# An attention-and-experts kernel: the first list's indices right behind their table's product, the next expert's gathers ahead of the puts

## The chip, the core and the metric

The kernel runs on one core of a Trainium2 chip, as one launch. The metric is the device time of that launch in microseconds (us). All tensors are drawn from a normal distribution, so which tokens go to which expert is known only while the kernel runs.

## The reference, cut to what matters

```python
# retention attention, batch 4, 8 heads, 768 steps, width 64
state = gamma * state + outer(k[t], v[t]);  y[t] = q[t] @ state / sqrt(64)
x = y as [3072, 512]
# mixture of experts, 8 experts, hidden width 1024
noisy = x @ w_gate + log1p(exp(x @ w_noise)) * noise
top2 = the two largest of noisy per token;  g = softmax over the two
for e in range(8):
    out[rows of e] += g * (relu(x[rows of e] @ w1[e]) @ w2[e])
```

What has to be computed is thus a causal recurrence over 768 steps for 32 head-batches, then a gate that sends each of the 3072 rows of x to two of eight experts, and for each expert two matrix products over its own rows.

## The kernel before, in words

**Stage one: attention.** Time is cut into chunks of 128 steps, 6 per batch, 24 in all. The loop over j at L677 handles one chunk per turn and is written so that several chunks are in flight. In turn j, TensorE gets the score products of the next chunk (`qk(j+1)`, L305), then what is listed for the turn in `between`, then the output products of this chunk (`y_mm(j)`, L320) and the gate logits of chunk j-3 (L360). VectorE scales the finished chunk j-1 in two halves (`x_hi` L345, `x_lo` L350) and multiplies the next chunk's scores by the causal mask (`masked`, L315). GpSimd scales v (`v_scale`, L282) and q (`q_scale`, L288). SyncE issues the loads, and for a finished chunk a transposing DMA and a store of its rows into `xbuf` (`x_out`, L354).

**Routing, hidden in the loop.** After each batch of 6 chunks its routing runs in steps (`route_a` to `route_g`), put into the turns by the lists `between` (before `y_mm`) and `todo` (behind it), filled at L634 to L670. `route_h` (L447) splits the gate values in two bf16 parts, `route_d` (L454) makes each token's slot, `route_e` one-hot matrices. `table(b)` (L507) multiplies them on TensorE, which gives each slot's token and gate in the PSUM region `LST`. `route_f` (L514) adds `LST` to `acc`, `slots` (L522) turns columns of `acc` into the row indices `idx`. `route_g` (L565) keeps copies of gates and places for a loop that serves overflowing lists at the end. `LST`, the places `POS` and the small sums `SUM` are regions of one PSUM tile, `pR` (L144 to L149). A Tile framework writes all semaphore waits; each engine's own order is the order of the calls.

**Weights of the first expert.** `w_load` to `w_lo` (L168 to L203) load one expert's weights, sum their squares on ScalarE, derive a scale (`w_scale`, a TensorE product into `SUM`, L184, and a VectorE reduction), and split them into two fp16 halves: ScalarE the upper (`w_hi`), VectorE the lower (`w_lo`), or ScalarE and GpSimd (`w_lo_pool`, L205). For expert 0 these steps are in the lists too.

**Stage two: experts.** `gather(e, t)` (L617) has GpSimd fetch 128 rows of `xbuf` by the indices, into one of four `xg` buffers; `x_t(e, t)` (L629) has SyncE issue the transposing DMA into `xe`, which waits for the gather. `mm1` (L716) is a first-product unit of 12 matmuls, with a relu on ScalarE and a remainder on VectorE; `mm2` (L748) a second-product unit of 24 matmuls; `put` (L742) has GpSimd add the scaled result `ot` to `out` by an indirect DMA. Puts go one behind the other: each waits for the landing of the one before. `ot` has four buffers.

**Expert 0 goes in pieces.** Its first list of 384 rows can only hold tokens of the first two batches, so its three gathers are possible once `route_f(1)` is done; they are in turns 21 and 22. When the loop is over, TensorE runs first-list units between the last routing steps (`early`, L787): eight `mm1` on 384 columns, three `mm2`, then eight `mm1` on columns 384 to 576, and one more `mm2`. At L840 four puts are issued; then SyncE reads the order of the other experts (L843) and issues 4 MB of loads for the next one (L844 to L846). The loop over experts starts at L849. For e = 0 it runs eight `mm1` on columns 576 to 832; `ahead` (L855) holds the seven gathers with transposes of the next expert, popped one per unit from the fifth unit on (L875) and then ahead of each `mm2` (L884).

Of the kernel before, what the change touches and what calls it, by code (L numbers as in the profile page):

```python
# [19 lines left out]
B, H, S, D = 4, 8, 768, 64  # L20
C = 128
NC = S // C
NCH = B * NC
# [11 lines left out]
B0 = B // 2  # L35
# [59 lines left out]
def moe_kernel(ctx, tc, qT, kT, kt, vt, noise, wgn, w1, w2, ctab, qtab, xbuf, out):  # L95
# [511 lines left out]
    def at(j, f, *a):  # L607
        todo.setdefault(j, []).append((f, a))
# [25 lines left out]
    between = {}  # L634
    for b in range(B - 1):
        n = (b + 1) * NC
        steps = [(2, route_a, b), (3, route_b, b), (4, route_b2, b), (4, route_c, b), (5, route_h, b), (5, route_d, b),
                 (6, route_e, b, 0), (7, route_e2, b, 0), (7, route_e, b, 1), (8, route_e2, b, 1), (9, route_f, b),
                 (8 if b == 0 else NCH - 1 - n, route_g, b)]
        if b == B - 2:  # L640
            steps = [(2, route_a, b), (3, route_b, b), (3, route_b2, b), (4, route_c, b), (4, route_h, b), (5, route_d, b)]
        else:
            between.setdefault(n + 9, []).append((table, b))
        between.setdefault(n + 5, []).append((places, b))
        for s in steps:
            at(n + s[0], *s[1:])
    at(0, gate_sum)
    at(1, gate_weights)
    for i in range(4):
        at((4, 7, 10, 12)[i], w_load, 0, "1", i)  # L650
        at((6, 9, 12, 14)[i], w_sum, 0, "1", i)
        at((15, 16, 17, 18)[i], w_hi, 0, "1", i)
        at((18, 19, 20, 20)[i], w_lo, 0, "1", i)
        at((14, 16, 17, 18)[i], w_load, 0, "2", i)
        at((16, 18, 19, 20)[i], w_sum, 0, "2", i)
        at(21 + i // 2, w_hi, 0, "2", i)
# [3 lines left out]
    between.setdefault(21, []).append((w_scale, 0, "2"))  # L660
    at(22, w_lo_pool, 0, "2", 0)
    between[NCH - 1].append((w_lo_pool, 0, "2", 1))
    at(NC * (B0 + 1) + 3, slots, 0, 3)
    for t in range(3):
        at(NC * (B0 + 1) + 3 + t // 2, gather, 0, t, 0, 128, B0 * S)
        if t < 2:
            at(NC * (B0 + 1) + 4, x_t, 0, t)
    between[NCH - 1].append((x_t, 0, 2))
    mid = SECOND // 128
    at(1, nc.sync.dma_start, xbuf[:128, :], zero.bitcast(F16))  # L670
# [32 lines left out]
    x_hi(NCH - 1)  # L703
    x_lo(NCH - 1)
    x_out(NCH - 1)
    for i in range(7):
        zero_out(i)
    lctx.close()
# [128 lines left out]
        early(2)  # L837
    early(len(units))
    out_scale(0, mid, NBLK)
    for t in range(mid):  # L840
        put(0, t, first[t])
    for r in range(E - 1):
        order.append(nc.sync.value_load(eid[0:1, r:r + 1], min_val=1, max_val=E - 1))  # L843
    for w in "12":  # L844
# [4 lines left out]
    for e in range(E):  # L849
        half = (CAPS[e] + 31) // 32 * 16  # L850
        cols = [(SECOND, CAPS[0])] if e == 0 else [(0, half), (half, CAPS[e])]
        n, more = 0, e + 1 < E

        if more:
            ahead = [lambda t=t: (gather(e + 1, t), x_t(e + 1, t)) for t in blocks(e + 1)]  # L855
        for n0, n1 in cols:
            for f in range(FT):
                mm1(e, n0, n1, f)
                if tail is not None and n == 0:
                    put(*tail[:2], tail_out(*tail))  # L860
                    tail = None
                if e:
                    if n == 2:
                        w_scale(e, "2")
                        out_scale(e, 0, NBLK)
                    if 3 <= n < 7:
                        w_hi(e, "2", n - 3)
                    if 4 <= n < 8:
                        w_lo(e, "2", n - 4)
                    if more and n == 2:  # L870
                        w_load(e + 1, "1", 0, 2)
                        w_load(e + 1, "1", 2, 2)
                if more and len(cols) * FT - 5 <= n < len(cols) * FT - 1:
                    w_sum(e + 1, "1", n - (len(cols) * FT - 5))
                if e == 0 and n >= 4:  # L875
                    ahead.pop(0)()
                n += 1
        if more and e:
            w_load(e + 1, "2", 0, 2)
            w_load(e + 1, "2", 2, 2)  # L880
            w_scale(e + 1, "1")
        todo = list(range(mid, NBLK)) if e == 0 else list(blocks(e))
        for n, t in enumerate(todo):
            if more and ahead:  # L884
                ahead.pop(0)()
            if block(e, t)[1] < 128:
                tail = mm2_tail(e, t)
            else:
                put(e, t, mm2(e, t))
                if tail is not None:  # L890
                    put(*tail[:2], tail_out(*tail))
                    tail = None
            if e == 0 and n == 0:
                w_scale(1, "1")
            if more:
                for i in ((2 * n, 2 * n + 1) if e == 0 else (n,)):
                    if i < 4:
                        w_hi(e + 1, "1", i)
                    if 1 <= i < 5:
                        w_lo(e + 1, "1", i - 1)  # L900
                if e and 2 <= n < 6:
                    w_sum(e + 1, "2", n - 2)
            if e == 1 and n == 2:
                route_g(b - 1)
                route_g(b)
                loop_table()
        if e == 0:
            for i in range(4):
                w_sum(1, "2", i)
# [102 lines left out]
```

## Time and profile before

| | |
|---|---|
| median of 3 runs | 712.27 us (711.22 to 712.94) |
| the profiled execution, its own time | 716.62 us |
| its span, first to last instruction | 714.2 us |
| TensorE matmul busy | 672.1 us, 94% |
| VectorE, ScalarE, GpSimd busy | 296.2, 298.2, 216.2 us |
| mean granted TensorE clock | 0.964 of full speed |

The page of the profile gives the busy time of each engine, the span in 40 slices with the granted TensorE clock, and the chain of work that ended last. The trace behind it gives single instructions in order of time (the timeline), the idle time in front of groups of instructions and who ended it (the waits), and busy time and clock in chosen stretches (the windows). Times in these views count from the start of the span. Stage one lasts until about 142 us, the first-list units start at about 151 us, and the next expert's units at about 231 us.

### The profile page before, as it was taken

Reading aid. Unit: us, or ns where it says so; the run is one execution under the profiler, and the core shown is the slowest. Engines: PE = TensorE matmul, PEld = TensorE weight load, DVE = VectorE, ACT = ScalarE, POOL = GpSimd, SP = SyncE. Lnnn points to the kernel's source line nnn. Section 1 sums busy time; section 2 is a strip of 40 time slices with the busy share of each in tenths; the row PEclk is TensorE's granted clock in tenths of the full one; section 3 lists DMA queues with packets and bytes.
Section 4 is the critical chain, followed back from the end, with each engine's and each line's share of the span. In section 5 each row is a group of like instructions: output and inputs, shape, how many; then the busy total and the mean of one; then the engine's idle time right before and its main releaser. Section 6 shows DMA issues by size and latency. Waiting matters only on the chain.

```text
span 714.2 us, 11981 instructions
## 1 busy us (share of the span) xinstructions
PE 672.1 (94%) x4789; PEld 420.2 (59%) x4789; DVE 296.2 (41%) x731; ACT 298.2 (42%) x540; POOL 216.2 (30%) x170
## 2 busy tenths in 40 slices
PE   8999999859897999999999999999999999999991
PEld 6999898735674554555455545554554465456540
DVE  4457879867733343453216220622152144215100
ACT  4543454721146453444344442444353454344110
POOL 3544445340515202420441043114312340330021
PEclk9999798969999899999999999999999999999997
DMA  9999999576489853675476367626671785462132
GB/s 335 321 309 359 350 315 288 132 238 236 98 243 201 194 164 68 124 197 133 77 138 208 94 117 123 218 60 125 109 271 30 132 185 158 73 116 47 16 44 31
DMA packets 116136, 119.22 MB, mean 167 GB/s; under 512 B 82608, under 2 KB 82864, under 8 KB 112496
## 3 DMA queue, kind: packets, MB, share of 16 engines
q1 hardware_dynamic: 104112, 91.25, 44.4%
q0 software_dynamic: 11392, 26.35, 20.4%
q8 instruction: 38, 0.62, 0.4%
q10 hardware_dynamic: 576, 0.85, 0.3%
q14 instruction: 18, 0.15, 0.1%
HBM read 72.80 MB, written 26.21 MB: 139 GB/s over the span
## 4 chain that ended last, share of the span: by engine, by line
PE 82%; DMA 6%; DVE 5%; issue 2%; ACT 2%; POOL 1%; SPq 1%; POOLq 0%; ACTq 0%
PE pH L725 12%; PE pH L723 12%; PE pH L724 12%; PE pO L753 11%; PE pO L755 11%; PE pO L754 11%; PE pY L325 4%; PE pA L311 2%; DMA out<-ot,idx 2%; PE pY L329 2%; PE pU L334 2%; DMA xg<-xbuf,idx 1%; DMA xe<-xg 1%; DVE am L318 1%; DMA in_v<-vt 1%
## 5 line engine op out<-in xcount | busy, mean ns | idle before, releaser
L744 POOL DMA_INDIRECT out<-ot,idx x54 | 85.8, 1589 | 357.7 <-ACT ot L739 232.2
L723 PE MATMUL pH<-xe,w1h 128*128 128x384 f16 (+4 forms) x544 | 177.9, 327 | 15.0 <-DMA xe<-xg 12.8
L724 PE MATMUL pH<-xe,w1h 128*128 128x384 f16 (+4 forms) x544 | 177.8, 327 | 0.0
L725 PE MATMUL pH<-xe,w1l 128*128 128x384 f16 (+4 forms) x544 | 177.5, 326 | 0.0
L727 DVE SCALAR_TENSOR_TENSOR hl<-pH,hh 128x384 f16<-128x384 f32 (+4 forms) x136 | 74.4, 549 | 220.2 <-ACT hh L726 199.7
L755 PE MATMUL pO<-w2h,hl 128*128 128x512 f16 x384 | 145.6, 379 | 0.0
L753 PE MATMUL pO<-w2h,hh 128*128 128x512 f16 x384 | 145.6, 379 | 0.0
L754 PE MATMUL pO<-w2l,hh 128*128 128x512 f16 x384 | 145.6, 379 | 0.0
L726 ACT ACTIVATE hh<-pH 128x384 f16<-128x384 f32 (+4 forms) x136 | 65.4, 483 | 139.1 <-PE pH L725 131.8
L739 ACT ACTIVATE ot<-pO,gse 128x512 f32<-128x512 f32 (+4 forms) x54 | 37.1, 686 | 174.4 <-PE pO L755 166.1
L202 DVE SCALAR_TENSOR_TENSOR w1l<-wst,wsc,w1h 128x1024 f16<-128x1024 f32 x32 | 41.7, 1313 | 99.0 <-ACT w1h L197 99.0
L723 PEld LDWEIGHTS <-w1h 128*128 128x128 f16 x544 | 54.3, 100 | 46.6 <-issue 10.3
L724 PEld LDWEIGHTS <-w1h 128*128 128x128 f16 x544 | 53.7, 99 | 35.9 <-issue 3.8
L725 PEld LDWEIGHTS <-w1l 128*128 128x128 f16 x544 | 53.8, 99 | 35.3 <-issue 2.2
L624 POOL DMA_INDIRECT xg<-xbuf,idx x55 | 56.7, 1030 | 55.7 <-DVE wacc L527 23.4
L180 ACT ACTIVATE junk<-wst 128x1024 bf16<-128x1024 f32 x64 | 67.1, 1048 | 0.9 <-DMA wst<-w 0.6
L755 PEld LDWEIGHTS <-hl 128*128 128x128 f16 x384 | 37.5, 98 | 45.3
L753 PEld LDWEIGHTS <-hh 128*128 128x128 f16 x384 | 38.1, 99 | 44.1
L754 PEld LDWEIGHTS <-hh 128*128 128x128 f16 x384 | 37.5, 98 | 44.0
L325 PE MATMUL pY<-vp,am 128*128 128x64 f32 x384 | 51.2, 290 | 2.1 <-DVE dn L433 2.0
L325 PEld LDWEIGHTS pY<-vp,am 128*128 128x128 f32 x384 | 47.9, 203 | 4.8 <-POOL vp L285 2.1
L285 POOL TENSOR_TENSOR vp<-in_v,ct 128x512 f32<-128x512 f32 x24 | 25.9, 1080 | 61.5 <-issue 24.5
(162 smaller groups left out, 713.1 us busy)
## 6 DMA issues: line engine op xcount, KB each, us to landing
wst<-w SPq DMA_DIRECT2D x28, 1024.0 KB
in_q<-qT SPq DMA_DIRECT2D x24, 256.0 KB
in_k<-kT SPq DMA_DIRECT2D x24, 256.0 KB
in_v<-vt SPq DMA_DIRECT2D x24, 256.0 KB
in_kt<-kt SPq DMA_DIRECT2D x24, 256.0 KB
xbuf<-x SPq DMA_DIRECT2D x24, 256.0 KB
out<-zero SPq DMA_DIRECT2D x6, 1024.0 KB
wst<-w SPq DMA_DIRECT2D x8, 512.0 KB
```

What stands on the lines that cost most here:

```text
L180: nc.scalar.activation(junk, st[:, i * 1024:(i + 1) * 1024], AF.Square, accum_out=ss[:, i:i + 1])
L325: nc.tensor.matmul(pY[:, 2 * i + s, :], AM[j][:, s, i, :], VP[j][:, 2 * i + s, :], start=(i == 0 and s == 0), stop=True, skip_group_check= ...
L624: nc.gpsimd.indirect_dma_start(out=x[:p1], out_offset=None, in_=xbuf[:128 + rows], in_offset=bass.IndirectOffsetOnAxis(ap=idx[:p1, i:i + 1 ...
L723: nc.tensor.matmul(p[:, :n], whi, xh, start=(k == 0), stop=False)
L724: nc.tensor.matmul(p[:, :n], whi, xl, start=False, stop=False)
L725: nc.tensor.matmul(p[:, :n], wlo, xh, start=False, stop=(k == KT - 1))
L726: nc.scalar.activation(hh[:, f, n0:n1], p[:, :n], AF.Relu)
L727: nc.vector.scalar_tensor_tensor(hl[:, f, n0:n1], p[:, :n], 0.0, hh[:, f, n0:n1], op0=OP.max, op1=OP.subtract)
L744: nc.gpsimd.indirect_dma_start(out=out, out_offset=bass.IndirectOffsetOnAxis(ap=idx[:n, i:i + 1], axis=0), in_=ot[:n], in_offset=None, com ...
L753: nc.tensor.matmul(p, a, WT["2h"][:, f, :], start=(f == 0), stop=False)
L754: nc.tensor.matmul(p, a, WT["2l"][:, f, :], start=False, stop=False)
L755: nc.tensor.matmul(p, c, WT["2h"][:, f, :], start=False, stop=(f == FT - 1))
```

## The change

Five things move; nothing is added to or taken from the work.

- `route_h` of the first two batches goes one turn earlier (n+4 instead of n+5).
- For batch 1 (`b == B0 - 1`), `route_f`, `slots` and the first two gathers leave the end of turn 21 and go into `between[21]`, directly behind `table(1)`. The product `w_scale(0, "2")`, which is in `between[21]` as well, then comes behind them. The third gather goes into `between[22]`, ahead of `y_mm(22)`.
- The last `w_lo` of the first weight goes from turn 20 to turn 22.
- `route_g(1)` goes from turn 23 to behind the last chunk's `x_out`.
- At the start of stage two only the first of the four early puts stays where it was. The seven gathers of the next expert are spread over the eight units of expert 0 as 2, 2, 0, 1, 0, 1, 0, 1, and the other three puts are issued behind the third, fifth and seventh unit.

```diff
@@ -634,14 +634,20 @@
     between = {}
     for b in range(B - 1):
         n = (b + 1) * NC
-        steps = [(2, route_a, b), (3, route_b, b), (4, route_b2, b), (4, route_c, b), (5, route_h, b), (5, route_d, b),
+        steps = [(2, route_a, b), (3, route_b, b), (4, route_b2, b), (4, route_c, b), (4, route_h, b), (5, route_d, b),
                  (6, route_e, b, 0), (7, route_e2, b, 0), (7, route_e, b, 1), (8, route_e2, b, 1), (9, route_f, b),
-                 (8 if b == 0 else NCH - 1 - n, route_g, b)]
+                 (8, route_g, b)]
         if b == B - 2:
             steps = [(2, route_a, b), (3, route_b, b), (3, route_b2, b), (4, route_c, b), (4, route_h, b), (5, route_d, b)]
         else:
             between.setdefault(n + 9, []).append((table, b))
         between.setdefault(n + 5, []).append((places, b))
+        if b == B0 - 1:
+
+            steps = steps[:-2]
+            between[n + 9] += [(route_f, b), (slots, 0, 3)]
+            between[n + 9] += [(gather, 0, t, 0, 128, B0 * S) for t in range(2)]
+            between.setdefault(n + 10, []).append((gather, 0, 2, 0, 128, B0 * S))
         for s in steps:
             at(n + s[0], *s[1:])
     at(0, gate_sum)
@@ -650,7 +656,7 @@
         at((4, 7, 10, 12)[i], w_load, 0, "1", i)
         at((6, 9, 12, 14)[i], w_sum, 0, "1", i)
         at((15, 16, 17, 18)[i], w_hi, 0, "1", i)
-        at((18, 19, 20, 20)[i], w_lo, 0, "1", i)
+        at((18, 19, 20, 22)[i], w_lo, 0, "1", i)
         at((14, 16, 17, 18)[i], w_load, 0, "2", i)
         at((16, 18, 19, 20)[i], w_sum, 0, "2", i)
         at(21 + i // 2, w_hi, 0, "2", i)
@@ -660,11 +666,8 @@
     between.setdefault(21, []).append((w_scale, 0, "2"))
     at(22, w_lo_pool, 0, "2", 0)
     between[NCH - 1].append((w_lo_pool, 0, "2", 1))
-    at(NC * (B0 + 1) + 3, slots, 0, 3)
-    for t in range(3):
-        at(NC * (B0 + 1) + 3 + t // 2, gather, 0, t, 0, 128, B0 * S)
-        if t < 2:
-            at(NC * (B0 + 1) + 4, x_t, 0, t)
+    for t in range(2):
+        at(NCH - 2, x_t, 0, t)
     between[NCH - 1].append((x_t, 0, 2))
     mid = SECOND // 128
     at(1, nc.sync.dma_start, xbuf[:128, :], zero.bitcast(F16))
@@ -703,6 +706,7 @@
     x_hi(NCH - 1)
     x_lo(NCH - 1)
     x_out(NCH - 1)
+    route_g(B0 - 1)
     for i in range(7):
         zero_out(i)
     lctx.close()
@@ -837,8 +841,7 @@
         early(2)
     early(len(units))
     out_scale(0, mid, NBLK)
-    for t in range(mid):
-        put(0, t, first[t])
+    put(0, 0, first[0])
     for r in range(E - 1):
         order.append(nc.sync.value_load(eid[0:1, r:r + 1], min_val=1, max_val=E - 1))
     for w in "12":
@@ -872,8 +875,12 @@
                         w_load(e + 1, "1", 2, 2)
                 if more and len(cols) * FT - 5 <= n < len(cols) * FT - 1:
                     w_sum(e + 1, "1", n - (len(cols) * FT - 5))
-                if e == 0 and n >= 4:
-                    ahead.pop(0)()
+                if e == 0:
+
+                    for g in range((2, 2, 0, 1, 0, 1, 0, 1)[n]):
+                        ahead.pop(0)()
+                    if n in (2, 4, 6):
+                        put(0, n // 2, first[n // 2])
                 n += 1
         if more and e:
             w_load(e + 1, "2", 0, 2)
```

## The prediction

> **What bounds the kernel now.** I read the page's busy times first, then TensorE's waits, then the timeline around each wait.
>
> ```profile
> PE 672.1 (94%) x4789; PEld 420.2 (59%) x4789; DVE 296.2 (41%) x731; ACT 298.2 (42%) x540; POOL 216.2 (30%) x170
> PE pH L723 <- DMA xe<-xg: 12.8, 2, 8.5
> PE pY L325 <- DVE dn L433: 2.0, 1, 2.0
> ```
>
> TensorE is busy 94% of the span, so only its gaps are to be had. The waits (total, times, longest) name the large ones: twice it stands before a first-product unit because the transposed rows are missing, 12.8 us in all, one time 8.5 and so the other 4.3. Both waits lie where the change works. The first, in the timeline:
>
> ```profile
> 125.27 3.48 DVE L202 SCALAR_TENSOR_TENSOR w1l<-wst,wsc,w1h 128x1024 f16<-128x1024 f32 x2
> 130.12 0.74 DVE L352 SCALAR_TENSOR_TENSOR x<-pY,upx,x 128x512 f16<-128x512 f32 x1
> 131.28 0.43 DVE L518 TENSOR_TENSOR acc<-acc,pR 128x280 f32<-128x280 f32 x1
> 134.81 0.16 DVE L528 TENSOR_TENSOR wacc<-wacc,acc 128x3 f32<-128x3 f32 x1
> 134.99 1.15 POOL L624 DMA_INDIRECT xg<-xbuf,idx  x1 [8.51 <-DVE wacc L528]
> 137.44 1.05 POOL L285 TENSOR_TENSOR vp<-in_v,ct 128x512 f32<-128x512 f32 x1
> 143.89 0.98 POOL L624 DMA_INDIRECT xg<-xbuf,idx  x1
> 144.23 0.57 SPq L358 DMA_DIRECT2D xbuf<-x  x1
> 147.68 3.04 DMA xe<-xg
> 150.86 0.48 PE L723 MATMUL pH<-xe,w1h 128*128 128x384 f16 x1 [8.54 <-DMA xe<-xg]
> ```
>
> Here the list's indices are ready at 135.0, the third gather is issued only at 143.89, SyncE issues its transpose at 147.68 and TensorE starts at 150.86. The second wait, in the chain that ended last and the timeline:
>
> ```profile
> 204.21 10.76 DMA out<-ot,idx
> 217.59 4.44 DMA xg<-xbuf,idx
> 222.23 1.29 SPq L631
> 226.90 3.94 DMA xe<-xg
> 230.97 0.50 PE pH L723
> 231.47 0.35 PE pH L724
> 197.78 0.21 DVE L534 SCALAR_TENSOR_TENSOR idx<-tk,padv 128x49 int32<-128x49 f32 x1
> 203.17 2.36 SPq L176 DMA_DIRECT2D wst<-w  x4
> ```
>
> The next expert's indices exist at 198.0, but GpSimd is held in the puts: the third, issued at 204.21, lands 10.76 us later beside the 4 MB of weight loads, the fourth waits for it, and the first gather follows at 217.59. The four transposes are issued from 222.23 and the last lands at 230.84.
>
> A wait costs more than its length, as the clock shows:
>
> ```profile
> 115.89 1.29 PE L311 MATMUL pA<-qs,in_k 64*128 64x128 f32 x14 [1.41 <-DVE am L318]
> 72.40:82.60 10.20, 9.75 (x58) 9.44 (x60) 9.91 (x14) 4.19 (x10) 3.65 (x3) 0.50 1.15 332
> 116.80:123.60 6.80, 6.80 (x34) 6.54 (x32) 6.77 (x10) 2.36 (x5) 2.29 (x2) 0.50 1.07 290
> 231.00:236.20 5.20, 5.20 (x17) 2.53 (x18) 0.33 (x1) 1.26 (x4) 1.84 (x2) 0.50 0.96 186
> ```
>
> The windows' last three columns are granted clock, DMA share and GB/s. After a wait of 1.41 us in the attention stage TensorE ran 6.8 us at half clock; another spell there lasted 10.2 us; after the 4.3 us wait the units ran at half clock for 5.2 us.
>
> **The change, part by part: the next expert's gathers.** Four gathers now stand behind the first put only. They can be issued from 198.0, each 1.15 us or less with a short gap behind it, so the fourth by about 203; a landing of 4.44 us puts it at 207.5. SyncE is held by its loads until 205.53 (203.17 + 2.36) and can then issue the transposes at once, 17 us sooner. But their data stand in the hardware queue behind the 4 MB of loads:
>
> ```profile
> 214.00:216.00 2.00, 2.00 (x11) 0.88 (x10) 0.42 (x1) 0.56 (x3) 0.28 (x1) 1.00 0.95 401
> 216.00:218.00 2.00, 2.00 (x11) 0.88 (x9) 0.00 (x0) 0.00 (x0) 1.70 (x2) 1.00 0.45 113
> 225.72 2.48 DVE L202 SCALAR_TENSOR_TENSOR w1l<-wst,wsc,w1h 128x1024 f16<-128x1024 f32 x2 [2.73 <-ACT w1h L197]
> 230.57 1.06 ACT L180 ACTIVATE junk<-wst 128x1024 bf16<-128x1024 f32 x1
> 211.83 1.06 ACT L180 ACTIVATE junk<-wst 128x1024 bf16<-128x1024 f32 x1 [0.60 <-DMA wst<-w]
> DMA to landing us min/median/max: 3.1/5.0/6.5
> ```
>
> The loads are through by about 216.7 (401 GB/s, then 113). Issued one behind the other before, the transposes took (226.90 - 222.23) / 3 = 1.56 us each, so four take 6.2 us and the last lands at about 223. TensorE comes free at 230.97 - 4.3 = 226.7, so the 4.3 us go, with 3.7 us to spare. Next late would be the weights' lower half, ready at 228.2, but a unit uses its last quarter only in its 12th matmul. At half clock one of these took 0.35 us, so a unit of 12 takes 2.1 us at full clock, and the 12th comes at 228.6. ScalarE's sums end at 231.6 and hold the first relu; with three `pH` buffers TensorE asks for the first one back at 226.7 + 3 x 2.1 = 233. The half-clock spell goes as well: 5.2 us at half speed is 2.6 us. This part: -4.3 - 2.6 = **-6.9 us**.
>
> The three puts fall behind gathers: the fifth gather waits until the first transpose frees its `xg` buffer, about 218.5 (216.7 + 1.56, rounded up), and the puts behind it land at about 226 and 231, at the 5.0 us that the last row of the fence has as the median of all puts. That costs nothing: the third `ot` is wanted by the tail's result only after the next expert's first unit, at about 229 to 232. The last gathers, about 228, and their transposes are wanted after eight units, 226.7 + 8 x 2.1 = 243.5.
>
> **The first list.** Three things move. The last `w_lo`, half of the 3.48 us or less (I take 1.3), leaves VectorE's queue ahead of `route_f`. `route_f` and `slots` stand right behind `x_lo` (ending at 130.86) instead of behind the next routing steps: L518 ends at 130.86 - 1.3 + 0.43 = 130.0 instead of 131.7, and the gathers start at about 131 instead of 135. The third gather goes ahead of GpSimd's `w_lo_pool` and needs only the indices; it lands by 140. Then not the gather but SyncE's own order is late: the third transpose stands behind `x_out(22)`, whose store ends its issue at 144.23 + 0.57 = 144.8. So 147.68 - 144.8 = 2.9 us are to be had, not 8.5.
>
> Against this stands a new wait. `w_scale(0, "2")` writes `SUM`, `route_f` reads `LST`, both parts of one PSUM tile. In program order the read came behind `w_scale`; now it is ahead of it. Does a region of `pR` wait for another?
>
> ```profile
> 168.78 0.30 PE L426 MATMUL pR<-mb,oneb 128*128 128x60 bf16 x6
> 174.11 1.59 PE L511 MATMUL pR<-bb,a 128*128 128x280 bf16 x12
> 175.74 0.22 DVE L459 TENSOR_TENSOR ov<-pR,cb 128x60 f32<-128x60 f32 x1 [1.63 <-PE pR L511]
> 127.06 0.39 PE L184 MATMUL pR<-wss,onef 128*128 128x4 f32 x2 [0.20 <-ACT junk L180]
> 135.12 1.06 PE L334 MATMUL pU<-vp,in_kt 128*128 128x128 f32 x8
> ```
>
> L459 reads the places, written by L426 at 169, and yet it stood 1.63 us until L511 had written the other region. So order is kept for the whole tile, and the product at 127.06 will stand until 130.0: **2.9 us** of TensorE, with `y_mm(21)`, `qk(23)` and `y_mm(22)` (ending at 136.18) queued behind it, and behind that `x_lo(22)`, `x_out(22)` and the third transpose. The Trainium skill says why a framework does this (PSUM — Partial Sum Buffer, "PSUM bank collisions raise a hardware error"): two engines in one bank at once are an error, reads and writes alike. No row here shows the case of a write behind a read; by that rule it waits too.
>
> So 2.9 us are won and 2.9 lost: nothing at full clock. Then the clock: a 2.9 us wait in the attention stage is longer than the 1.41 us that brought half clock. The cost is between 0 (clock holds) and 5.1 (half of 10.2); I take half of the 6.8 us spell, the nearest in place, 3.4, since about 9 us of TensorE work remain up to the end of `y_mm(22)` (127.06 to 136.18). This part: 0 + 3.4 = **+3.4 us**; the first unit starts at about 154.3.
>
> **At nothing:**
>
> ```profile
> 67.76 1.27 DVE L451 CAST vv<-gr 128x12 bf16<-128x12 f32 x1
> 144.31 2.78 DVE L574 TENSOR_SCALAR t<-t 128x60 f32<-128x60 f32 x1
> 155.27 0.56 DVE L727 SCALAR_TENSOR_TENSOR hl<-pH,hh 128x384 f16<-128x384 f32 x1 [4.20 <-ACT hh L726]
> 60.00:75.00 15.00, 12.83 (x143) 12.07 (x141) 12.58 (x39) 5.61 (x14) 7.09 (x7) 0.91 1.11 348
> ```
>
> `route_h` stands one mask product earlier in VectorE's queue. It delays one mask by up to about 1.3 us (L451 is its longest step) and shortens the way to the next by as much; the DMA engines are full there (share 1.11), so TensorE can't run ahead for long. Bounds -1.3 to +1.3. `route_g(1)`, with its 2.78 us step, moves into the 4.20 us in which VectorE stands idle before L727; without that cover it would cost those 2.8 us. The moved `v_scale(23)` no longer stands behind gathers until 137.44, so the 2.0 us wait before `y_mm(23)` goes, but that chunk ends long before the first unit and gains nothing.
>
> **Sum.** -6.9 + 3.4 = -3.5 us. The profiled execution would take 713.1 instead of 716.62; the median of the runs shown lies 4.35 us under that profile, and 712.27 - 3.5 = 708.8.
>
> **The rivals.** *The clock holds.* The Trainium skill (TensorE: Matmul & The Clock Gate, "HAM oscillation — how this bites in real kernels") says that gaps above about 3.4 us must be avoided; by that rule a 2.9 us wait costs no clock. With the clock held, the first list costs nothing and the sum is -6.9: 705.4. Against it stand the 1.41 us wait and its 6.8 us at half clock. 0.14.
>
> *The new wait isn't there.* If regions of `pR` are told apart for a write behind a read, TensorE runs on and 2.9 us are won: -2.9 - 6.9 = -9.8, 702.5. L459 speaks against it. 0.07.
>
> *The transposes get among the weight loads.* They are now issued at 205.5, while the loads run. If the DMA engines take them in turns with the loads instead of behind them, the loads end up to 6.2 us later. ScalarE sums their squares in its queue ahead of relus, so those come late, and TensorE's buffers cover about 2.6 us of it (two units on 256 instead of 416 columns, 1.3 each). The rest, 3.6, is a new wait, again with 2.6 of clock: 6.2, and only 0.7 of the 6.9 is left. With the first list's +3.4 the sum is +2.7: 715.0, slower. It decides from the point where the sum of squares that began at 211.83 begins later than 214.4. For it speaks that SyncE had always issued these transposes after the loads were through; against it that loads and transposes share one queue. 0.15.
>
> *Only half of the second wait goes*, as the transposes land at 225 to 229 (slower behind loads than 1.56 us each): about zero. 0.06. The forecast keeps 0.58; 0.04 of it, with the 10.2 us spell, lies within 0.2%.
>
> **How the numbers follow.** 0.2% is 1.4 us, about what a measurement of this kernel can tell from no change. Faster: 0.54 + 0.14 + 0.07 = 0.75; within: 0.04 + 0.06 = 0.10; slower: 0.15. The forecast's own range is 707 to 711 (clock cost 1.7 to 5.1). 703.5 to 714.0 takes in the holding clock and the half-gone wait and leaves out most of the 0.07 and 0.15.
>
> **What would show it.** Right: L184 in front of `y_mm(21)` starts only when L518 has ended, with TensorE idle for about 3 us and at half clock after; the third transpose directly behind the store L358; the first L723 of expert 0 later than 150.9; no wait before the next expert's L723 and full clock there. Wrong: L184 still at about 127, a first unit before 149, or ScalarE's L180 waiting long for `wst`.

## The result, and the profile after

| | before | after |
|---|---|---|
| median of 20 runs each | 712.88 us (708.69 to 720.78) | 709.16 us (706.24 to 713.89) |
| ratio, 95% interval | | 0.9949 (0.9930 to 0.9967) |
| the profiled execution, its own time | 716.62 us | 709.86 us |
| its span | 714.2 us | 707.6 us |
| mean granted TensorE clock | 0.964 | 0.970 |

The change makes the kernel 3.7 us faster; 3.5 us were forecast. All ratios here are estimated from the runs in the chip's faster state alone, against runs of the kernel before on the same chip (its median is 712.9 to 718.0 us from chip to chip), so they differ a little from the quotients of the medians. In the code after the change the lines up to L633 keep their numbers; `mm1`'s products are L727 to L729 (before L723 to L725), its remainder L731, `put` L748.

The page's busy times after the change:

```profile
PE 670.5 (95%) x4789; PEld 420.5 (59%) x4789; DVE 299.2 (42%) x731; ACT 298.4 (42%) x540; POOL 220.6 (31%) x170
```

TensorE is busy for 1.6 us less and the span is 6.6 us shorter, so gaps went. Its waits (us in total, times, longest us), those that bear on the change:

```profile
PE pH L727 <- DMA xe<-xg: 7.8, 1, 7.8
PE pR L184 <- DVE acc L518: 3.7, 1, 3.7
PE pH L727 <- DVE hl L731: 1.1, 1, 1.1
```

One of the two waits for transposed rows is gone, the next expert's. The first list's is still there, 7.8 instead of 8.5 us, and a wait that the kernel before did not have stands in the second row: TensorE's product of the weight sums, L184, waits for VectorE's read of the table, L518. The timeline around the first list:

```profile
127.20 1.60 PE L511 MATMUL pR<-bb,a 128*128 128x280 bf16 x12
131.95 0.43 DVE L518 TENSOR_TENSOR acc<-acc,pR 128x280 f32<-128x280 f32 x1
132.53 0.35 PE L184 MATMUL pR<-wss,onef 128*128 128x4 f32 x2 [3.72 <-DVE acc L518]
132.74 3.09 PE L325 MATMUL pY<-vp,am 128*128 128x64 f32 x16
133.32 1.15 POOL L624 DMA_INDIRECT xg<-xbuf,idx  x1 [4.71 <-DVE wacc L528]
140.68 0.97 POOL L624 DMA_INDIRECT xg<-xbuf,idx  x1
143.68 1.06 PE L334 MATMUL pU<-vp,in_kt 128*128 128x128 f32 x8
152.04 0.57 SPq L358 DMA_DIRECT2D xbuf<-x  x1
152.70 1.30 SPq L631 DMA_TRANSPOSE xe<-xg  x1
155.91 0.48 PE L727 MATMUL pH<-xe,w1h 128*128 128x384 f16 x1 [7.84 <-DMA xe<-xg]
```

L184 starts 0.15 us after the end of L518. `y_mm(21)` behind it takes 3.09 us for what took 1.98 us before: most of it runs at half clock. The third transpose is issued at 152.70, directly behind the store L358 (152.04 + 0.57 = 152.61). The windows of the two half-clock spells there (the last three columns are granted clock, DMA share, GB/s):

```profile
133.40:140.30 6.90, 6.90 (x44) 6.81 (x45) 2.70 (x28) 0.88 (x3) 2.85 (x3) 0.51 0.53 152
150.40:160.70 10.30, 4.79 (x23) 2.42 (x24) 9.27 (x20) 4.41 (x7) 7.07 (x4) 0.50 0.60 161
```

The first begins 0.9 us after the new wait's end and covers most of `y_mm(21)` and `qk(23)`; the second comes with the wait for the rows. The second part of the change, in the timeline of GpSimd, SyncE, ScalarE and TensorE:

```profile
198.44 1.63 POOL L748 DMA_INDIRECT out<-ot,idx  x1 [0.30 <-issue]
201.65 1.00 POOL L624 DMA_INDIRECT xg<-xbuf,idx  x1 [1.58 <-DVE capd L562]
206.99 0.96 POOL L624 DMA_INDIRECT xg<-xbuf,idx  x1 [0.32 <-issue]
208.15 2.52 SPq L176 DMA_DIRECT2D wst<-w  x4
210.79 30.40 SPq L631 DMA_TRANSPOSE xe<-xg  x7
214.89 1.06 ACT L180 ACTIVATE junk<-wst 128x1024 bf16<-128x1024 f32 x1 [2.69 <-DMA wst<-w]
218.98 1.06 ACT L180 ACTIVATE junk<-wst 128x1024 bf16<-128x1024 f32 x1 [1.36 <-DMA wst<-w]
226.04 1.50 POOL L624 DMA_INDIRECT xg<-xbuf,idx  x1 [16.17 <-DMA xe<-xg]
231.42 0.34 PE L727 MATMUL pH<-xe,w1h 128*128 128x416 f16 x1
```

The next expert's first unit starts at 231.42 with no wait and at full clock (0.34 us a matmul, 0.50 before), as the window shows that answers to 231.00:236.20 of before:

```profile
231.40:236.60 5.20, 5.20 (x38) 3.10 (x35) 1.66 (x2) 5.07 (x11) 2.54 (x2) 1.00 0.78 155
```

Its four gathers are out by 206.99 and SyncE turns to its transposes right behind the loads, but the rows land late all the same: the fifth gather, which needs the first transpose's buffer, waits until 226.04.

**Stretches.** Two executions of one kernel differ by several us in places that the change doesn't touch: from the next expert's first second-product to the end it took 446.18 us before and 441.70 us after, with the same instructions, and in two experiments that contain the second part 446.1 and 446.6 us. So I compare three stretches that hold the change: A from the start of `table(1)`'s products L511 to the first list's first unit, B from there to the next expert's first unit, C from there to that expert's first second-product. Before, these four points lie at 125.26, 150.86, 230.97 and 268.02 us, after at 127.20, 155.91, 231.42 and 265.90.

| kernel | A | B | C | sum | ratio to before (95%) |
|---|---|---|---|---|---|
| before | 25.60 | 80.11 | 37.05 | 142.76 | |
| after | 28.71 | 75.51 | 34.48 | 138.70 | 0.9949 (0.9930 to 0.9967) |
| only the puts | 25.60 | 75.39 | 34.47 | 135.46 | 0.9878 (0.9832 to 0.9923) |
| only the list | 26.26 | 80.75 | 36.98 | 143.99 | 1.0042 (1.0013 to 1.0072) |
| scale first | 24.01 | 76.62 | 34.47 | 135.10 | 0.9895 (0.9839 to 0.9951) |
| filled wait | 25.57 | 75.69 | 34.48 | 135.74 | 0.9881 (0.9837 to 0.9925) |
| changed, again | 26.24 | 77.33 | 34.48 | 138.05 | 0.9964 (0.9928 to 1.0000) |
| scale first, again | 24.95 | 77.19 | 34.47 | 136.61 | 0.9893 (0.9843 to 0.9943) |
| early transposes | 17.85 | 83.33 | 34.47 | 135.65 | 0.9898 (0.9874 to 0.9923) |
| late copies | 15.82 | 80.70 | 34.47 | 130.99 | 0.9866 (0.9841 to 0.9891) |
| late copies and slots | 15.48 | 81.54 | 34.48 | 131.50 | 0.9858 (0.9830 to 0.9886) |
| spread | 16.24 | 76.88 | 34.47 | 127.59 | 0.9826 (0.9789 to 0.9863) |
| only the puts, again | 25.58 | 74.02 | 34.48 | 134.08 | 0.9901 (0.9872 to 0.9929) |

After against before the sum is 4.06 us smaller: +3.11 in A, -4.60 in B, -2.57 in C. The rest of the 6.6 us between the two spans is -4.48 us behind C, which is such drift, and +1.94 us ahead of L511, which need not be: the change moves `route_h` there. The ten traces that hold the list reach L511 at 125.7 to 132.4 us, the three without it at 125.3 to 126.2. What the list costs ahead of A these stretches leave out, and no run moves `route_h` alone.

### The profile page after: what moved, and what is told of

Read it like the earlier page. It is cut to its first block, busy times and chain, and to the rows that moved or that the text cites. A ratio compares the mean times of both kernels' runs of the same rounds, so it can differ in the third digit from the quotient of the medians.

```text
span 707.6 us, 11981 instructions
## 1 busy us (share of the span) xinstructions
PE 670.5 (95%) x4789; PEld 420.5 (59%) x4789; DVE 299.2 (42%) x731; ACT 298.4 (42%) x540; POOL 220.6 (31%) x170
## 4 chain that ended last, share of the span: by engine, by line
PE 82%; DVE 8%; DMA 4%; SPq 2%; ACT 2%; issue 1%; POOL 0%; POOLq 0%; ACTq 0%
PE pH L727 12%; PE pH L728 12%; PE pH L729 12%; PE pO L757 11%; PE pO L759 11%; PE pO L758 11%; PE pY L325 4%; PE pA L311 2%; PE pU L334 2%; PE pY L329 2%; DVE am L318 2%; DMA in_v<-vt 1%; DMA wst<-w 1%; DVE x L352 1%; DVE w1l L202 1%
## 5 line engine op out<-in xcount | busy, mean ns | idle before, releaser
L748 POOL DMA_INDIRECT out<-ot,idx x54 | 85.5, 1583 | 330.2 <-ACT ot L743 197.2
L727 PE MATMUL pH<-xe,w1h 128*128 128x384 f16 (+4 forms) x544 | 176.4, 324 | 9.0 <-DMA xe<-xg 7.8
L729 PE MATMUL pH<-xe,w1l 128*128 128x384 f16 (+4 forms) x544 | 176.4, 324 | 0.0
L731 DVE SCALAR_TENSOR_TENSOR hl<-pH,hh 128x384 f16<-128x384 f32 (+4 forms) x136 | 74.3, 549 | 205.2 <-ACT hh L730 205.2
L727 PEld LDWEIGHTS <-w1h 128*128 128x128 f16 x544 | 54.0, 99 | 41.3 <-issue 9.1
L729 PEld LDWEIGHTS <-w1l 128*128 128x128 f16 x544 | 53.4, 98 | 34.5 <-issue 0.9
## 6 DMA issues: line engine op xcount, KB each, us to landing
out<-zero SPq DMA_DIRECT2D x6, 1024.0 KB, 10.2
```

Source lines behind the costliest of these rows:

```text
L727: nc.tensor.matmul(p[:, :n], whi, xh, start=(k == 0), stop=False)
L729: nc.tensor.matmul(p[:, :n], wlo, xh, start=False, stop=(k == KT - 1))
L731: nc.vector.scalar_tensor_tensor(hl[:, f, n0:n1], p[:, :n], 0.0, hh[:, f, n0:n1], op0=OP.max, op1=OP.subtract)
L748: nc.gpsimd.indirect_dma_start(out=out, out_offset=bass.IndirectOffsetOnAxis(ap=idx[:n, i:i + 1], axis=0), in_=ot[:n], in_offset=None, com ...
```

## The experiments

The theory A is that of the prediction: the puts bring some 7 us, the list costs some 3, because the earlier read of the table makes TensorE wait in a stage where a wait costs half clock as well. The rivals put gain or loss elsewhere. Each kernel's edit is against the kernel before or after, as the heading says.

### Only the puts (against before)

```diff
-    for t in range(mid):
-        put(0, t, first[t])
+    put(0, 0, first[0])
...
-                if e == 0 and n >= 4:
-                    ahead.pop(0)()
+                if e == 0:
+                    for g in range((2, 2, 0, 1, 0, 1, 0, 1)[n]):
+                        ahead.pop(0)()
+                    if n in (2, 4, 6):
+                        put(0, n // 2, first[n // 2])
```

> The kernel before with the second part alone: the next expert's gathers ahead of the puts, nothing moved in the attention stage. Theory A (the prediction's): the wait of 4.3 us before the next expert's units and its half-clock spell go whole, -6.9 us against before, ratio 0.990. Theory B (the two parts are each half of what was said: the moved transposes slow the weight loads and eat half of the gain, and the first list costs nothing): -3.5 us, ratio 0.995, with ScalarE's L180 waiting some us for wst.

Measured: 708.55 us against 718.03, ratio 0.9878 (0.9832 to 0.9923). B and C are 7.30 us shorter, A is the same to the hundredth. So the second part alone is worth all of the gain and more, and the list must cost something. The waits for rows in this kernel:

```profile
PE pH L723 <- DMA xe<-xg: 9.2, 1, 9.2
```

One wait is left, the first list's.

### Only the list (against after)

```diff
-    put(0, 0, first[0])
+    for t in range(mid):
+        put(0, t, first[t])
...
-                if e == 0:
-                    for g in range((2, 2, 0, 1, 0, 1, 0, 1)[n]):
-                        ahead.pop(0)()
-                    if n in (2, 4, 6):
-                        put(0, n // 2, first[n // 2])
+                if e == 0 and n >= 4:
+                    ahead.pop(0)()
```

> The changed kernel with the puts and gathers of the next expert back in their old order: the first part alone. Theory A: the wait of L184 for L518 (about 3 us) and the half clock behind it cost more than the earlier gathers bring: +3.4 us against before, ratio 1.005, first unit of expert 0 at 153 to 156 us of the span. Theory B: 0, ratio 1.000.

Measured: 720.81 us, ratio 1.0042 (1.0013 to 1.0072): slower, 3.0 us of 718. The new wait is there in the timeline:

```profile
136.71 0.36 PE L184 MATMUL pR<-wss,onef 128*128 128x4 f32 x2 [2.77 <-DVE acc L518]
136.93 2.07 PE L325 MATMUL pY<-vp,am 128*128 128x64 f32 x16
```

Here `y_mm(21)` starts at nearly full clock (2.07 us), and the half clock comes only later, for one short spell:

```profile
138.70:142.00 3.30, 3.30 (x17) 3.30 (x17) 1.67 (x19) 0.00 (x0) 0.98 (x1) 0.50 0.76 230
```

So in this trace the wait of 2.77 us brought 3.4 us of half clock, and A is only 0.66 us longer; in the trace of after, 3.72 us brought 6.8 us, and A is 3.11 us longer. In A the list thus costs between 0.7 and 3.1 us in the traces, and in the times 3.0 us (0.9 to 5.2). The two need not be the same cost: this trace starts L511 7.08 us later than that of before.

### Scale first (against after)

```diff
-    between.setdefault(21, []).append((w_scale, 0, "2"))
+    between[21].insert(1, (w_scale, 0, "2"))
```

The product into `SUM` again comes ahead of the read of `LST` in program order, all else as after.

> The changed kernel with one line moved: the product w_scale(0, 2) goes ahead of route_f again, directly behind table(1). Theory A: the wait of L184 for L518 is gone, TensorE keeps the full clock, the third transpose is issued about 2.9 us earlier than in the kernel before: -2.9 - 6.9 = -9.8 us against before, ratio 0.986, some 6 us faster than the changed kernel. Theory B: the wait was harmless, since TensorE stands before the first unit anyway: as the changed kernel, ratio 0.995.

Measured: 710.73 us, 0.9895 (0.9839 to 0.9951), and in a later comparison 0.9893 (0.9843 to 0.9943). No wait for L518 is left, so that wait does come from the order of L184 and `route_f`. But the 9.8 us of the rival without the wait are not reached: A is 1.6 us shorter than before, not 2.9, and B is 1.2 us longer than with the puts alone. In A the trace shows why: TensorE stood 2.97 us for a mask just ahead of L511 and had half clock from 130.3 to 133.7 us, and L511 itself took 2.83 us instead of 1.60. The second trace of this kernel, in the section after the next, meets another wait at the same place.

### The wait filled (against after)

```diff
-    between.setdefault(21, []).append((w_scale, 0, "2"))
+    between[21] += [(busy, 13), (w_scale, 0, "2")]
```

Thirteen products on constants, which nothing reads, stand where TensorE would wait.

> The changed kernel with 13 products that nobody reads (128x512 bf16, some 0.22 us each) put ahead of w_scale(0, 2), so that TensorE works while it would wait for L518. Work is added, none left out. If the clock is what the wait costs (theory A), the spell of half clock behind it goes and the first unit comes 3.4 us earlier than in the changed kernel: -6.9 us against before, ratio 0.990. If the order alone costs and not the clock, it is as the changed kernel or some tenths slower: ratio 0.995.

Measured: 709.35 us, 0.9881 (0.9837 to 0.9925). The wait is nearly covered, and the clock stays at full speed from there to the end of the attention stage, as timeline and windows show:

```profile
126.15 1.60 PE L511 MATMUL pR<-bb,a 128*128 128x280 bf16 x12
127.59 2.97 PE L112 MATMUL pY<-warm 128*128 128x512 bf16 x13
131.47 0.36 PE L184 MATMUL pR<-wss,onef 128*128 128x4 f32 x2 [0.91 <-DVE acc L518]
131.68 1.98 PE L325 MATMUL pY<-vp,am 128*128 128x64 f32 x16
```

```profile
126.00:148.00 22.00, 16.97 (x164) 14.55 (x163) 16.02 (x73) 13.53 (x26) 8.44 (x8) 1.00 0.57 152
```

L184 comes 5.3 us after L511 (131.47 - 126.15), as late as after the change (132.53 - 127.20); from there on the clock differs, and A is 25.57 instead of 28.71 us. So 3.1 us of A in the trace of after are the clock, and the wait itself is balanced by the earlier third transpose, as the prediction had it. The ratio is that of the puts alone: with the clock held the list is worth nothing that these runs can tell, to about half a per cent.

### The change again, scale first again, and early transposes

The first two are the kernels above, run beside the third, so that all three share their runs of the kernel before.

> The changed kernel itself once more, beside the two below on one chip. -3.5 us against before by the prediction, ratio 0.995.

> The run with w_scale(0, 2) ahead of route_f again, repeated beside the changed kernel. Theory A: 6.3 us faster than the changed kernel (2.9 of waiting, 3.4 of half clock), -9.8 us against before, ratio 0.986. Theory C (the wait only takes the place of a wait that comes later before the first unit): 2 us or less faster than the changed kernel. From the start of the table's product L511 to the first unit of expert 0, which leaves out what happens earlier in the attention stage: 22.7 us by theory A, 25.6 or more by theory C; the kernel before has 25.6 and the changed one 28.7.

The change again: 714.27 us against 717.41, 0.9964 (0.9928 to 1.0000), again with a wait of 2.77 us at L184, with one short spell of half clock behind it and A at 26.24. Scale first: 711.25 us, 0.9893 (0.9843 to 0.9943); A is 24.95, between the 22.7 of theory A and the 25.6 of theory C. There L184 waits for ScalarE instead:

```profile
128.87 0.39 PE L184 MATMUL pR<-wss,onef 128*128 128x4 f32 x2 [1.56 <-ACT junk L180]
```

The sum of squares that L184 adds up is late by 1.56 us in this trace (0.20 us before), a spell of half clock follows from 131.5 to 134.9 us, and such waits vary from trace to trace; and its first-list units wait 1.8 us for remainders where those of the puts alone wait 1.1. Theory A's size for this kernel fell; its mechanism, that L518 no longer holds L184, did not.

Early transposes, against scale first: all three gathers in turn 21, all three transposes at the end of that turn, ahead of the stores of the chunks behind it.

```diff
-            between[n + 9] += [(gather, 0, t, 0, 128, B0 * S) for t in range(2)]
-            between.setdefault(n + 10, []).append((gather, 0, 2, 0, 128, B0 * S))
+            between[n + 9] += [(gather, 0, t, 0, 128, B0 * S) for t in range(3)]
...
-    for t in range(2):
-        at(NCH - 2, x_t, 0, t)
-    between[NCH - 1].append((x_t, 0, 2))
+    for t in range(3):
+        at(NCH - 3, x_t, 0, t)
```

> As the run before, and further: all three gathers of the first list stand directly behind slots in between[21], and their three transposes at the end of turn 21, ahead of x_out(21) and x_out(22) in SyncE's queue. If SyncE's order is what is late once the wait is gone (theory A), the wait before the first unit goes down from 7 us to 2 or less, L511 to the first unit is about 18 us, the half clock at its start goes too, and the kernel is 12 to 16 us faster than before, ratio about 0.980. If the indices or the weights were what is late (theory C), it is as the run with w_scale first.

Measured: 710.76 us, 0.9898 (0.9874 to 0.9923), not the 0.980 of theory A: no better than scale first. Yet A fell by 7.1 us, to 17.85, and the first unit waits only 0.65 us for its rows. B gave 6.1 us back. The timeline of ScalarE, VectorE and TensorE shows where:

```profile
152.83 0.15 DVE L157 TENSOR_SCALAR upx<-p2m 128x1 int32<-128x1 int32 x1
153.60 2.18 ACT L209 ACTIVATE wst<-wst,wsc 128x1024 f32<-128x1024 f32 x2
155.68 1.24 ACT L728 ACTIVATE hh<-pH 128x384 f16<-128x384 f32 x3
157.05 2.02 DVE L574 TENSOR_SCALAR t<-t 128x60 f32<-128x60 f32 x1
159.24 0.55 DVE L729 SCALAR_TENSOR_TENSOR hl<-pH,hh 128x384 f16<-128x384 f32 x1
159.84 0.48 PE L725 MATMUL pH<-xe,w1h 128*128 128x384 f16 x1 [6.03 <-DVE hl L729]
```

The first units start at 146.7, but their relus and remainders stand behind the attention's last steps: the scale of the last chunk (L157) comes only at 152.83, then ScalarE's weight copies, then the relu at 155.68, then `route_g(1)`, whose last steps hold VectorE up to the remainder at 159.24. TensorE has three buffers and waits 6.03 us for the first to come free. The prediction had named the 4.20 us of idle VectorE as the cover of `route_g`; here that cover is gone.

### Late copies, and late copies and slots (against early transposes, and one on the other)

```diff
-    route_g(B0 - 1)
...
+    route_g(B0 - 1)
     logits(NCH - 1)
     route_a(b)
```

> The kernel with the early transposes again, with one step moved: route_g(1), VectorE's copies of gates and places, stands behind the fourth first-product unit instead of right behind the last chunk. In the profile of the early transposes the first relu L728 ran at 155.68 and took about 0.49 us, but its remainder L729 began only at 159.24, since route_g's five steps (154.41 to 159.32) stood ahead of it on VectorE; TensorE's fourth unit waited 6.03 us for it, until 159.84. Theory A (the cover that my prediction named for route_g is gone once the first unit starts early): the remainder begins at about 156.2 and TensorE goes on at about 156.8, so the wait shrinks from 6.0 to about 3.0 us and the way from the first unit to the next expert's first unit from 83.3 to about 80.3; the time is about 0.5% under that of the early transposes: ratio to the kernel before 0.985. Rival B (the remainder waits for the relu, and route_g only filled the gap): the wait stays at 5 us or more, ratio 0.990.

```diff
-            steps = [(2, route_a, b), (3, route_b, b), (3, route_b2, b), (4, route_c, b), (4, route_h, b), (5, route_d, b)]
+            steps = [(2, route_a, b), (3, route_b, b), (3, route_b2, b), (4, route_c, b), (4, route_h, b)]
...
+    early(1)
+    route_d(b - 1)
     w_lo_pool(0, "2", 2)
     w_lo_pool(0, "2", 3)
-    early(1)
```

> As the kernel with the late copies, and two more steps are moved behind the first unit: route_d of the third batch (VectorE, 148.58 to 152.68 in the profile of the early transposes, ahead of the scale upx of the last chunk) and the two w_lo_pool copies (ScalarE, 2.18 us from 153.60, ahead of the first relu). Theory A: ScalarE's x_hi of the last chunk no longer waits 3.53 us for upx and no copy stands ahead of the relu, so the first relu runs at about 151 and TensorE's fourth unit has no wait over 1 us; the half clock that followed the wait (158.5 to 164.5, worth 3.0 us) goes as well. From the first unit to the next expert's first unit it is 83.3 - 6.0 - 3.0 = about 74 to 77 us, ratio to the kernel before 0.978 to 0.982. Rival B (the units are only the first in a row of late things: the second list's chain of products, slots and gathers sets the time of the following units whatever the first ones do): the wait goes, but another of 3 us or more appears between 160 and 225 us, and the ratio stays at 0.986 or above.

Measured: 704.77 and 704.60 us against 714.10, ratios 0.9866 (0.9841 to 0.9891) and 0.9858 (0.9830 to 0.9886). With the copies late the first wait shrinks to 2.87 us, about as expected. But another of 3.42 us appears behind the next remainder, and with the slots late as well a single one of 4.50 us, with B 0.8 us longer: much as rival B had it for the second kernel, whose ratio lies between those of the two theories (0.982 at most and 0.986 at least). In its timeline of VectorE and TensorE:

```profile
151.79 0.55 DVE L728 SCALAR_TENSOR_TENSOR hl<-pH,hh 128x384 f16<-128x384 f32 x1
152.63 2.15 DVE L463 SCALAR_TENSOR_TENSOR ov<-ov,sl 128x60 f32<-128x60 f32 x1
159.28 1.97 DVE L501 TENSOR_TENSOR bb<-ob,vv 128x1008 bf16<-128x1008 bf16 x2
161.17 1.48 DVE L728 SCALAR_TENSOR_TENSOR hl<-pH,hh 128x384 f16<-128x384 f32 x3
161.77 0.48 PE L724 MATMUL pH<-xe,w1h 128*128 128x384 f16 x1 [4.50 <-DVE hl L728]
```

The first remainder is now on time, at 151.79. From 152.25 to 161.17 VectorE does the third batch's slots and one-hot products in one row, and the second remainder stands behind them. Is it VectorE's order or its load?

### Spread, and only the puts again

Spread is the kernel with late copies and slots, with two units between the slots and the one-hot products, so that the row is cut in two. One of ScalarE's two weight copies thereby comes behind these units as well:

```diff
     early(1)
     route_d(b - 1)
     w_lo_pool(0, "2", 2)
+    early(2)
     w_lo_pool(0, "2", 3)
     logits(NCH - 3)
     route_e(b - 1, 0)
     products(b - 1, 0, nc.vector, 3, NV)
     early(1)
     logits(NCH - 2)
-    early(2)
```

> As the kernel with the late copies and the late route_d, but with two first-product units more between route_d and route_e of the third batch, and none between the second logits and route_g (the number of units ahead of the first gate sums stays eight). There VectorE did route_d, route_e and the products in one row from 152.25 to 161.17, 8.9 us, with the second remainder behind them at 161.17; TensorE waited 4.50 us for it and had half clock from about 159.3 to 166.4. Now the second and third remainder stand between the two rows, 5.6 and 3.3 us long, each shorter than the 6 us that three units take. Theory A (the gain of the early first list was given back only by VectorE's order): no wait for L728 over 1.5 us up to 166 us and no half clock there; from the first unit to the next expert's first unit 81.5 - 4.5 - 3.5 = about 73.5 us, ratio to the kernel before 0.975 to 0.980. Rival B (VectorE's whole work between 148 and 190 us is what sets the time of the units, not its order): the wait comes back behind a later unit, the stretch stays at 78 us or more, ratio 0.984 or above.

> The kernel before with only the second part of the change, run again beside the spread kernel on one chip, so that what the first list is worth at its best can be read as the difference of two kernels. Its first unit follows the table's product by 25.6 us as before, and from there to the next expert's first unit it takes 75.4 us. Both theories expect a ratio to the kernel before of 0.988 to 0.990. If theory A holds for the spread kernel, that one is about 1% faster than this (16 + 73.5 us against 25.6 + 75.4 us, 11 us less); if B holds, by less than 0.5%.

Measured, side by side: 701.18 us for the spread, 705.40 for the puts alone, 713.49 for the kernel before; ratios 0.9826 (0.9789 to 0.9863) and 0.9901 (0.9872 to 0.9929). The waits of the spread kernel behind its first unit:

```profile
PE pH L724 <- DVE hl L728: 2.3, 1, 2.3
```

The wait of 4.50 us is down to 2.26, with half clock only from about 154.7 to 158.2 us, and B is 76.88 us, under the 78 that rival B set as the least. So a good part of the wait came from the order, though the edit moves one of ScalarE's copies with it. Theory A's 73.5 us for B and its ratio of 0.975 to 0.980 were not quite reached, since the row of the slots, 147.52 to 153.24, still held the next remainders for longer than TensorE's buffers last. This kernel is faster than the puts alone too, by 0.6% (701.18 / 705.40 = 0.994, and the two intervals don't meet), between the 1% of theory A and the 0.5% of rival B.

## Why the prediction was right, point by point

**The second part, -6.9 us.** The 4.25 us wait went and the half clock of the next expert's units with it. B is 4.60 us shorter and C 2.57 us, 7.2 in all; the 2.6 us of clock were measured to the tenth. B agrees in part by chance: it also lost a wait of 2.19 us for a remainder (at 195.62 before), got a new one of 1.10 (at 216.82 after), and its first units had half clock for 1.3 us longer. Alone, this part gave 7.3 us in the stretches, and ratios of 0.9878 and 0.9901 (712.27 - 6.9 would be 0.990).

**Inside that part, three times were off and cost little.** The second gather waited for the capacities (L562) and the third for a buffer of the second list, so the fourth was out at 206.99; behind the loads that doesn't matter. The transposes were slower behind the loads than I said: the fifth gather came 17.9 us after the loads' issue (226.04 - 208.15), not 15.3 (218.5 - 203.17). And the third rival was there in small. The first sum of squares came 6.7 us after the loads' issue (214.89 - 208.15), after a wait of 2.69 us, and the third 10.8 us after it, where it had been 8.7 (211.83 - 203.17); the rival was to decide from 11.2 (214.4 - 203.17). A window over the place shows what that cost TensorE:

```profile
215.00:217.00 2.00, 0.90 (x9) 0.65 (x7) 0.42 (x1) 2.00 (x4) 0.00 (x0) 1.00 1.06 335
```

TensorE is busy for 0.90 of the 2 us: 1.1 us of wait for a remainder (the wait for `hl` in the list of waits), at full clock, not the 6.2 us of the rival. Loads 2.2 us later thus cost 1.1 us here; that the cover of two units took the rest is argued, not shown. The two traces of the puts alone have no such wait at this place.

**The new wait, 2.9 us.** It measured 3.5 (3.72 against 0.20 before). The read L518 started 4.75 us after L511, where the prediction had it end at 4.74 (130.0 - 125.26); the moved `w_lo` brought `x_lo` forward by 0.8 us and not by 1.3. That a write of one region waits for the read of another was argued from L459 only; the runs now show it directly, at 3.72 and twice at 2.77 us, and gone when the order is turned back. This agrees with the rule of the Trainium skill that the prediction cited (PSUM — Partial Sum Buffer, "PSUM bank collisions raise a hardware error"), which has software guard a bank against two engines at once, reads and writes alike.

**The gain of the third transpose, 2.9 us.** It stands directly behind the store, 0.09 us after its end, where it had been 2.88 us behind it. This step held exactly: the gather is no longer what the third transpose waits for.

**The clock, +3.4 us.** The last product of `y_mm(22)` (L334) starts 16.48 us after L511, before 9.86 us: 6.62 us later. Of these 3.5 are the wait and 3.1 the clock, and the filled wait takes just these 3.1 away. On the way to the store another 0.75 us was won (8.36 instead of 9.11 us from L334 to L358), so A grew by 6.62 - 0.75 - 2.88 + 0.12 (small gaps) = 3.11 us, against +3.4 in the sum. But 3.1 us is one trace. In the two others the wait of 2.77 us cost 0.7 us in A; the median over 20 runs, -3.7 us against -7.1 and -8.7 for the puts alone (0.99 and 1.22% of 712.9), fits the larger size or more, and the second comparison of the change, 0.9964 (0.9928 to 1.0000), doesn't tell them apart.

**What was put at nothing.** `route_h` was bounded at 1.3 us either way. Up to `y_mm(20)` it is all that tells the list's kernels from before, and there the traces differ by more. The wait of 2.17 us for a mask at 72.85, with its 10.2 us of half clock, is gone in all ten (0.4 us at most is left). In its place TensorE waits 3.1 to 3.6 us for the first weight's sum of squares, at 88 to 92 us (2.2 us at most without the list), and 1.8 us for a mask at about 107 (none without). L511 then comes 0.4 to 7.1 us later than before. The times of the filled wait, which has the moved `route_h` too, leave little room for a lasting price, 0.9881 against 0.9878 for the puts alone; without a run that moves it alone this stays open. The total of -3.7 against -3.5 is thus partly luck: the mechanisms of the two parts were right, but the cost of the list, +3.4 in the sum, is anything from 0.7 us (A in two traces) to 5.0 (the medians, 8.7 - 3.7).

**The rival of the holding clock fell.** By the rule that was cited for it (the Trainium skill, TensorE: Matmul & The Clock Gate, "HAM oscillation — how this bites in real kernels") only gaps above about 3.4 us are to be avoided. The trace with the list alone disagrees: there 2.77 us was enough for a spell of 3.4 us. The filled kernel shows what the rival would have given, 0.9881.

## What to carry to other kernels

Where a framework writes the waits as here, a read that is moved ahead of a write of the same PSUM tile makes the writing engine wait, even where the regions differ; before moving one, look at what is next on the tile and what is queued behind it. When a wait is shortened, look for the work that had been hiding in it on other engines: here 7 us of earlier start were worth nothing until VectorE's steps behind it were moved, which cut TensorE's longest wait for a remainder from 6.03 to 2.26 us. And judge such a change by stretches between instructions of the trace rather than by whole spans, which differ by more than the change in places that it doesn't touch; but look ahead of the stretches for steps that moved there too.

## What the runs showed of the hardware that was not expected

The clock changes on a fixed grid. In the trace of before it went down or up at about 72.4, 82.65, 116.8, 123.6, 140.7, 154.3, 229.4 and 236.25 us, and all distances are multiples of 3.41 us; the same holds within every other trace, at another offset. A spell therefore lasts 3.4, 6.8, 10.2 or 13.7 us, and what a wait costs can depend on where it falls on the grid. The two traces of the changed kernel meet the same wait for a mask. First the trace of after, then that of the change again:

```profile
107.73 1.16 PE L311 MATMUL pA<-qs,in_k 64*128 64x128 f32 x14 [1.79 <-DVE am L318]
109.50:116.30 6.80, 6.80 (x47) 6.49 (x46) 6.59 (x17) 2.83 (x6) 2.11 (x2) 0.50 0.86 235
```

```profile
108.18 1.16 PE L311 MATMUL pA<-qs,in_k 64*128 64x128 f32 x14 [1.78 <-DVE am L318]
109.00:121.00 12.00, 8.93 (x96) 8.35 (x92) 11.76 (x26) 5.79 (x11) 7.58 (x5) 1.00 0.83 220
121.01 1.99 PE L311 MATMUL pA<-qs,in_k 64*128 64x128 f32 x14 [2.98 <-DVE am L318]
```

In the first, all but 0.1 us of the wait lies in one step of the grid (106.06 to 109.47), and two steps of half clock follow. In the second, a border at 107.47 splits it into 1.07 and 0.71 us, and the clock stays; TensorE then runs ahead into a wait of 2.98 us, with 10.2 us of half clock behind it, and reaches L511 at 131.86 instead of 127.20. All ten traces with the list divide so at this wait: six have it almost whole in one step, with a spell of 6.8 us behind it; four have it split, with no spell there but the later one of 10.2 us. It is no rule for every wait: in the trace of scale first again, 1.56 us split in halves brought a spell, and in that of the spread kernel 1.71 us at 125.6 us, almost whole in one step, brought none.

The Trainium skill (TensorE: Matmul & The Clock Gate, "What's actually happening") gives a free-running window of 3413 ns, with which the grid agrees, and at least one busy window before full speed; with the list alone one window was enough (TensorE busy for 3.30 of 3.30 us), while the spell behind the new wait after the change lasted two although TensorE was busy for all of it (6.90 of 6.90 us).
